# A pooled-attention and mixture-of-experts kernel: another place for the second lane's first weight loads, and a small table made on another engine at another slot

## The chip, the cores and the metric

The kernel runs on one core of one Trainium2 chip. The metric is device time in microseconds of one execution, from the first to the last instruction with what lies around it; less is better.

## The reference

```python
def _attn_ref(q, k, v):            # 8 batches, 8 heads, 576 positions, head size 64
    k_p = k.reshape(B, H, S // 8, 8, D).mean(axis=3)
    v_p = v.reshape(B, H, S // 8, 8, D).mean(axis=3)
    attn = softmax(q @ k_p.T / sqrt(D))
    return attn @ v_p
def _moe_ref(x, w_in, w_out):      # 4608 tokens, 512 -> 2048 -> 512
    h = x @ w_in
    return np.maximum(0.01 * h, h) @ w_out
def _moe2_ref(x, w_gate, w1, w2):  # 8 experts, 512 -> 1024 -> 512
    logits = x @ w_gate
    expert_idx = np.argmax(logits, axis=1)
    gate_w = softmax(logits)[np.arange(N), expert_idx]
    for e in range(E):
        xe = x[expert_idx == e]
        out[expert_idx == e] = gate_w[expert_idx == e, None] * (np.maximum(xe @ w1[e], 0) @ w2[e])
    return out
```

The output of each part, laid out as 4608 tokens of 512 numbers, is the input of the next.

## The kernel before

**Stages.** The tokens go through attention and the dense layer in 18 blocks of 256. The work of a block is 16 slots: in a slot `g1` makes 128 columns of the hidden layer (12 matmuls of 256 columns) and `g2` adds those of an earlier slot to the output (6 matmuls of 512 columns). Each operand is split in a high and a low part, and three of the four products are kept. The first two blocks share 40 slots; while they run, `w_conv1` and `w_conv2` turn the dense weights, which come as 64-bit numbers, into such pairs, on VectorE and ScalarE. All else (attention of later tokens, the routing, the loading and splitting of the experts' weights) is hung on the slots: `at(slot, function)` puts a function in a list, and `run_slot` calls the list of the slot, in the order of the `at` calls, right after the slot's `g1`. The code is written out as each engine's queue, and every engine works through its queue in order.

**Routing.** After each block `route_a` to `route_c` pick the expert of every token and scatter the token's number into a list `lst` in DRAM, by an indirect DMA of GpSimd. `early` picks the expert with most tokens before the last block is counted; four tiles of 128 of its tokens (pairs 0 and 1) start at once.

**The expert stage.** It works on pairs of tiles; a pair has eight slots, again 12 matmuls of 256 columns (`p_g1`) and 6 of 512 (`p_g2`). Slots are counted from 0 anew, so pair p has slots 8p to 8p+7. Weights of experts lie in two lanes of SBUF, four pieces of 2 MB each (`w_load`; pieces 0 and 1 are the first layer, 2 and 3 the second). Pairs 0, 1 and 2 use lane 0, pair 3 is the first that uses lane 1. `w_next` reloads a piece after its last use, with a condition: if the next step of that lane has the same expert, the load is skipped. All these loads are issued by SyncE, in the order of its queue, with the expert's number read from the table `itab` into a register (`value_load`, `w_regs`).

While pair 1 runs, the last block is routed and the plan for the other pairs is made: `final` (slot 5) computes each step's expert with the per-step constants `stepc`; `fetch` (slot 6) reads the token lists; `final_list` (slot 8) writes `itab`; `unpack` (slot 10) makes `gidx`, `sidx` and `gate`, the rows to gather, the rows to write and the factors. Then `p_gather(2)` and `p_gather(3)` issue four indirect gathers on GpSimd, 128 rows each into the two halves of a tile, and `p_xT(2, 0)` and `p_xT(2, 1)` (slots 14 and 15) transpose what came on TensorE, with a copy on ScalarE and a subtraction on VectorE. `m_out` scales a tile's result and scatters it into `out`, by an indirect DMA of GpSimd; a pair has two of them, and the second waits until the first has landed.

**What the change touches.** In slot 8, `final_3` reads the registers of lane 1's first step and issues its pieces 0 and 1. In slot 10, `final_4` issues the four gathers, then has SyncE read one element of `gidx`, and then issues pieces 2 and 3. `step_consts`, in slot 36 of the first stage, makes the six columns of `stepc` from the partition's number: an iota on GpSimd and 29 instructions on VectorE, of one element in each of 128 partitions. `stepc` is read for the first time by `final`.

Of the kernel before, what the change touches and what calls it, by code (L numbers as in the profile page):

```python
# [15 lines left out]
ALU = mybir.AluOpType  # L16
# [5 lines left out]
def kernel(  # L22
# [12 lines left out]
    nc = tc.nc  # L35
    P = 128
    B, H, S, D = q.shape
    NT, DM = out.shape
# [14 lines left out]
    NE = 4  # L53
# [3 lines left out]
    NPS = 12  # L57
    NEP = NE // 2
    FT = NE + 2 * NPS
    NSS = NPS + NSTEP - FT  # L60
# [51 lines left out]
    def sb(shape, dt, tag, bufs=1):  # L112
        return pool.tile(shape, dt, name=tag, tag=tag, bufs=bufs)
# [11 lines left out]
    def f32(ap):  # L125
        return ap.bitcast(F32)
# [4 lines left out]
    def sub(eng, o, a, b):  # L131
        eng.tensor_tensor(out=o, in0=a, in1=b, op=ALU.subtract)  # L132
# [486 lines left out]
    gidx = pool.tile([P, NSTEP], I32, name="gidx")  # L619
# [5 lines left out]
    itab = pool.tile([P, NR + 1, 2], I32, name="itab")  # L625
# [20 lines left out]
    def unpack(L, n, c0):  # L646
        p = pt("att")
        for j in range(2):
            nc.tensor.transpose(p[:, j * 64:j * 64 + n], L[0:n, :, j], ident[0:n, 0:n])
        cs = slice(c0, c0 + n)  # L650
        nc.vector.tensor_copy(sidx[:, cs], p[:, 0:n])
        nc.vector.tensor_scalar(
            out=gidx[:, cs], in0=p[:, 0:n], scalar1=float(NT - 1), scalar2=None, op0=ALU.min
        )
        nc.vector.tensor_copy(gate[:, cs], p[:, 64:64 + n])
# [76 lines left out]
    def final_list(cv):  # L732
        V = nc.vector
        p = pt("att")
        for j in range(2):
            nc.tensor.matmul(
                p[0:1, j * 64:j * 64 + NR], cv[0:NR, j:j + 1], ident[0:NR, 0:NR], start=True, stop=True
            )
        er, ch = etab[0:1], sb([1, NSS], F32, "fch")
        V.tensor_copy(er[:, 2:2 + NPS], p[0:1, 0:2 * NPS:2])  # L740
        V.tensor_copy(er[:, 2 + NPS:2 + NSS], p[0:1, 2 * NPS:NR])
        V.tensor_copy(itab[0:1, 0:NSS, 0], er[:, 2:2 + NSS])
        i = 0
        while i < NSS:
            j = i + 1
            while j < NSS and prev_of(j) - prev_of(i) == j - i:
                j += 1
            a = 2 + prev_of(i)
            V.tensor_tensor(out=ch[:, i:j], in0=er[:, 2 + i:2 + j], in1=er[:, a:a + j - i], op=ALU.not_equal)
            i = j  # L750
        V.tensor_copy(itab[0:1, 0:NPS, 1], ch[:, 0:NPS])
        V.tensor_tensor(
            out=itab[0:1, NPS:NSS, 1], in0=ch[:, NPS:], in1=p[0:1, 64 + 2 * NPS:64 + NR], op=ALU.mult
        )

    def step_consts():
        V = nc.vector
        pi = sb([P, 4], I32, "spi")
        pf = sb([P, 6], F32, "spf")
        j, mem, od, t, x, ns = [pf[:, i:i + 1] for i in range(6)]  # L760
        T, isp, thr, ng, du, c5 = [stepc[:, i:i + 1] for i in range(6)]

        def ts(o, i, a, op0, b=None, op1=None):
            kw = {} if op1 is None else {"op1": op1}
            V.tensor_scalar(out=o, in0=i, scalar1=a, scalar2=b, op0=op0, **kw)

        nc.gpsimd.iota(pi[:, 0:1], pattern=[[0, 1]], base=0, channel_multiplier=1)
        V.tensor_copy(j, pi[:, 0:1])
        ts(pi[:, 1:2], pi[:, 0:1], 1, ALU.bitwise_and)
        V.tensor_copy(mem, pi[:, 1:2])  # L770
        ts(pi[:, 2:3], pi[:, 0:1], 1, ALU.arith_shift_right, 1, ALU.bitwise_and)
        V.tensor_copy(od, pi[:, 2:3])
        ts(pi[:, 3:4], pi[:, 0:1], 2, ALU.arith_shift_right)
        V.tensor_copy(t, pi[:, 3:4])
        ts(isp, j, float(2 * NPS), ALU.is_lt)
        ts(ns, isp, -1.0, ALU.mult, 1.0, ALU.add)
        ts(od, od, float(NPS // 2), ALU.mult)
        V.tensor_tensor(out=t, in0=t, in1=od, op=ALU.add)
        ts(x, j, -2.0 * NPS, ALU.add)
        for q, to in ((4, 6), (5, 4), (6, 7), (7, 5)):  # L780
            ts(od, j, float(2 * NPS + q), ALU.is_equal, float(to - q), ALU.mult)
            V.tensor_tensor(out=x, in0=x, in1=od, op=ALU.add)
        sub(V, t, t, x)
        V.scalar_tensor_tensor(out=T, in0=t, scalar=isp, in1=x, op0=ALU.mult, op1=ALU.add)
        V.scalar_tensor_tensor(out=thr, in0=T, scalar=2.0 * NPS, in1=ns, op0=ALU.add, op1=ALU.mult)
        ts(ng, isp, -1.0, ALU.mult, -1.0, ALU.add)
        ts(du, ns, 2.0, ALU.mult)
        V.tensor_tensor(out=mem, in0=mem, in1=isp, op=ALU.mult)
        V.tensor_tensor(out=c5, in0=T, in1=ng, op=ALU.mult)
        sub(V, c5, mem, c5)  # L790
        ts(c5, c5, -float(E * CAP), ALU.add)
# [47 lines left out]
    def w_load(ln, pieces, e, cond):  # L839
        for pc in pieces:  # L840
            kw = {} if cond is None else {"cond": cond}
            nc.sync.dma_start(
                out=f32(wt[ln, pc].rearrange("p c (h n) -> p c h n", h=2)),
                in_=wsp[bass.ds(e, 1), pc].rearrange("o p c h n -> p (o c) h n"),
                **kw,
            )

    regs = {}

    def w_regs(s):  # L850
        e = nc.sync.value_load(itab[0:1, s, 0:1], min_val=0, max_val=E - 1)
        c = nc.sync.value_load(itab[0:1, s, 1:2], min_val=0, max_val=1) if s < NSS else None
        regs[s] = (e, c)
# [13 lines left out]
    def p_gather(p):  # L867
        x = sb([P, 2, DM], F32, "ps", 3)
        for i in range(2):
            m_gather(2 * p + i, x[:, i])  # L870
# [136 lines left out]
    def at(slot, fn, *a):  # L1007
        hooks.setdefault(slot, []).append((fn, a))
# [97 lines left out]
    with tc.manual_schedule():  # L1106
# [70 lines left out]
            at(o, fn, t)  # L1177
        at(LAG, att_av, 1)
        at(31, prefill)
        at(36, step_consts)  # L1180
        at(20, lambda: nc.sync.dma_start(out=wgk, in_=moe2_w_gate.rearrange("(k p) e -> p k e", p=P)))
        at(27, gate_rows)
        at(4, q_load, 4)
# [16 lines left out]
        for s, (b, f) in enumerate(seq):  # L1200
# [19 lines left out]
            if (b, f) == (1, NF - 1):  # L1220
# [4 lines left out]
                    out=wg_t[0].rearrange("p e d -> p (e d)"),  # L1225
# [26 lines left out]

        def final_3():
            final_list(fin["cv"])
            w_regs(1)
            w_load(1, [0, 1], *regs[1])

        def final_4():
            unpack(early_list.pop(0), NR, NE)
            p_gather(NEP)  # L1260
            p_gather(NEP + 1)
            nc.sync.value_load(gidx[0:1, NE:NE + 1], min_val=0, max_val=NT - 1)
            w_load(1, [2, 3], *regs[1])

        at(0, y_tr, b, 0)
        at(1, y_tr, b, 1)
# [7 lines left out]
        at(5, final_1)  # L1274
        at(6, final_2)
        at(8, final_3)
        at(10, final_4)
        at(14, p_xT, 2, 0)
        at(15, p_xT, 2, 1)
        for p in range(NEP, NEP + NPS):  # L1280
            if p + 2 < NEP + NPS:
                at(8 * p + 1, p_gather, p + 2)
# [86 lines left out]
```

## Time and profile before

| | us |
|---|---|
| median of three runs | 1557.83 (1556.98 to 1558.25) |
| the profiled execution, its own time | 1558.05 |
| its span, first to last instruction | 1556.0 |
| TensorE busy, share of the span | 1472.8, 95% |
| VectorE busy | 939.4, 60% |
| ScalarE busy | 626.8, 40% |
| GpSimd busy | 327.3, 21% |

PE is TensorE's matmuls, PEld its weight loads, DVE is VectorE, ACT ScalarE, POOL GpSimd, SP SyncE; a q behind a name is that engine's sequencer. L900 is line 900 of the kernel. Times in the rows are microseconds from the span's start; the text behind the operation is out<-in by the program's names. A row of the timeline may merge several instructions (x12); its first number is the start of the first, its second reaches to the end of the last. What stands in brackets is the engine's idle time before the row, and what ended it.

### The profile page before, as it was taken

Reading aid. Unit: us, or ns where it says so; the run is one execution under the profiler, and the core shown is the slowest. Engines: PE = TensorE matmul, PEld = TensorE weight load, DVE = VectorE, ACT = ScalarE, POOL = GpSimd, SP = SyncE. Lnnn points to the kernel's source line nnn. Section 1 sums busy time; section 2 is a strip of 40 time slices with the busy share of each in tenths; the row PEclk is TensorE's granted clock in tenths of the full one; section 3 lists DMA queues with packets and bytes.
Section 4 is the critical chain, followed back from the end, with each engine's and each line's share of the span. In section 5 each row is a group of like instructions: output and inputs, shape, how many; then the busy total and the mean of one; then the engine's idle time right before and its main releaser. Section 6 shows DMA issues by size and latency. Waiting matters only on the chain. (4 is left out here: it accounts for less than half of the span.)

```text
span 1556.0 us, 25769 instructions
## 1 busy us (share of the span) xinstructions
PE 1472.8 (95%) x9272; PEld 1317.6 (85%) x9272; DVE 939.4 (60%) x2468; ACT 626.8 (40%) x1442; POOL 327.3 (21%) x294
## 2 busy tenths in 40 slices
PE   3698989999999999999999999999799999999998
PEld 3586879999898888899989989988699999998887
DVE  6998658879778878877877977664122121211111
ACT  4676434544444454444444444322122222222222
POOL 4000012232232233222222332121212111111111
PEclk8699999999999999999999999999899999999999
DMA  9443135555544545535645644143511117566160
GB/s 216 148 132 100 63 99 190 167 188 169 169 167 166 182 149 185 184 140 171 197 153 157 203 149 163 48 178 122 245 41 55 35 48 300 211 257 259 41 250 24
DMA packets 121386, 238.06 MB, mean 153 GB/s; under 512 B 56845, under 2 KB 65041, under 8 KB 117544
## 3 DMA queue, kind: packets, MB, share of 16 engines
q1 hardware_dynamic: 90312, 139.81, 28.7%
q10 hardware_dynamic: 23328, 76.56, 13.0%
q0 software_dynamic: 7616, 20.01, 3.8%
q8 instruction: 75, 1.23, 0.3%
q14 instruction: 55, 0.45, 0.1%
HBM read 317.78 MB, written 87.38 MB: 260 GB/s over the span
## 5 line engine op out<-in xcount | busy, mean ns | idle before, releaser
L526 PE MATMUL y<-w,ghl 128*128 128x512 f32 x1728 | 466.3, 406 | 2.8 <-DVE ghl L132 2.5
L526 PEld LDWEIGHTS y<-w,ghl 128*128 128x128 f32 x1728 | 310.1, 192 | 61.7 <-DVE ghl L132 6.3
L132 POOL TENSOR_TENSOR ps<-ps 128x512 f32<-128x512 f32 x128 | 181.6, 1419 | 482.2 <-ACT ps L129 361.8
L498 PEld LDWEIGHTS h<-x_t,w 128*128 128x128 f32 x1776 | 239.6, 195 | 39.8 <-DVE w L132 16.9
L498 PE MATMUL h<-x_t,w 128*128 128x256 f32 x1776 | 246.4, 288 | 24.0 <-DVE w L132 15.3
L546 DVE CUSTOM_DVE_ANT_0 junk<-y,wg 128x512 bf16<-128x512 f32 x256 | 200.3, 783 | 1.9
L498 PEld LDWEIGHTS y<-x_t,w 128*128 128x128 f32 x1488 | 193.2, 189 | 9.6
L498 PE MATMUL y<-x_t,w 128*128 128x256 f32 x1488 | 196.1, 282 | 0.0
L935 PE MATMUL y<-w,ghl 128*128 128x512 f32 x672 | 176.5, 401 | 0.9 <-DVE ghl L923 0.9
L935 PEld LDWEIGHTS y<-w,ghl 128*128 128x128 f32 x672 | 120.4, 190 | 22.4 <-DVE ghl L923 1.3
L129 ACT ACTIVATE g<-h 128x256 f32<-128x256 f32 x164 | 63.0, 384 | 145.9 <-PE h L498 132.8
L991 POOL DMA_INDIRECT out_dram<-kv,sidx x40 | 40.1, 1003 | 382.5 <-ACT kv L990 199.3
L923 DVE SCALAR_TENSOR_TENSOR ghl<-h,ghl 128x256 fp32r<-128x256 f32 x56 | 23.8, 425 | 135.9 <-ACT ghl L922 135.9
L506 DVE TENSOR_TENSOR h<-g,h 128x256 f32<-128x256 f32 x132 | 56.0, 424 | 77.7 <-ACT g L129 77.2
L132 DVE TENSOR_TENSOR at_t<-a,at_t 128x512 fp32r<-128x512 f32 x62 | 42.7, 688 | 87.6 <-ACT at_t L129 87.2
L129 ACT ACTIVATE ghl<-h 128x256 fp32r<-128x256 f32 x132 | 50.7, 384 | 92.9 <-PE y L526 42.8
L129 ACT ACTIVATE ps<-ps 128x512 fp32r<-128x512 f32 x128 | 80.5, 629 | 17.8 <-DMA ps<-in_moe_w_dram 8.7
L129 ACT ACTIVATE ghl<-y 128x256 fp32r<-128x256 f32 x124 | 47.3, 382 | 95.2 <-DVE y L506 50.5
L132 DVE TENSOR_TENSOR x_t<-a,x_t 128x512 fp32r<-128x512 f32 x60 | 41.1, 688 | 51.7 <-ACT x_t L129 51.7
L129 ACT ACTIVATE g<-y 128x256 f32<-128x256 f32 x124 | 47.4, 382 | 60.9 <-PE y L498 53.4
L295 DVE TENSOR_TENSOR kv<-kv 72x512 f32<-72x512 f32 (+8 forms) x126 | 68.0, 540 | 3.2
L613 POOL DMA_INDIRECT lst<-ent,six x36 | 37.8, 1051 | 150.4 <-DVE six L612 115.1
(291 smaller groups left out, 2157.2 us busy)
## 6 DMA issues: line engine op xcount, KB each, us to landing
w<-wsp SPq DMA_DIRECT2D x108, 2048.0 KB
wsp<-ps ACTq DMA_DIRECT2D x128, 512.0 KB
ps<-in_moe_w_dram SPq DMA_DIRECT2D x128, 256.0 KB
y_d<-y ACTq DMA_DIRECT2D x18, 512.0 KB
q<-in_q_dram SPq DMA_DIRECT2D x28, 256.0 KB
kv<-in_k_dram SPq DMA_DIRECT2D x24, 288.0 KB
kv<-in_v_dram SPq DMA_DIRECT2D x24, 256.0 KB
ps<-in_moe_w_in_dram SPq DMA_DIRECT2D x8, 512.0 KB
```

Of the source, the lines that this page charges most:

```text
L129: nc.scalar.activation(o, i, AF.Copy, scale=scale)
L132: eng.tensor_tensor(out=o, in0=a, in1=b, op=ALU.subtract)
L295: eng.tensor_tensor(out=o, in0=t[:, :, 0:w], in1=t[:, :, w:2 * w], op=ALU.add)
L498: nc.tensor.matmul(p[:, 0:BLK], win(f)[:, kk, l], xv[:, kk, r], start=(n == 0), stop=(n == 3 * KD - 1))
L506: nc.vector.tensor_tensor(out=g, in0=t, in1=h, op=ALU.max)
L526: nc.tensor.matmul(y_ps[b, i], hl[:, l, i * P:i * P + P], wout(f)[:, r], start=(f == 0 and l + r == 0), stop=(last and l == 1),)
L546: nc.vector.tensor_tensor_reduce(out=jk, in0=y_sb[b][:, i], in1=wg_t[0][:, e], scale=1.0, scalar=0.0, op0=ALU.mult, op1=ALU.add, accum_out ...
L613: nc.gpsimd.indirect_dma_start(out=lst, out_offset=bass.IndirectOffsetOnAxis(ap=ix[:, 0:1], axis=0), in_=ent[:, i, :], in_offset=None, bou ...
L923: nc.vector.scalar_tensor_tensor(out=hl[:, 1], in0=b, scalar=0.0, in1=f32(hl[:, 0]), op0=ALU.max, op1=ALU.subtract)
L935: nc.tensor.matmul(o_ps[2 * p + i], hl[:, l, i * P:i * P + P], w[:, r], start=(f == 0 and l + r == 0), stop=(f == 7 and l == 1),)
L991: nc.gpsimd.indirect_dma_start(out=out, out_offset=bass.IndirectOffsetOnAxis(ap=sidx[:, t:t + 1], axis=0), in_=o, in_offset=None, bounds_c ...
```

## The change

Three things are done.

1. `first_load`, a new function in slot 12, takes the place of the four loads in slots 8 and 10. It sets one element of `itab` on VectorE, has SyncE read that element, reads the registers of lane 1's first step and issues all four pieces. In VectorE's queue the new instruction stands right behind the subtraction of `p_xT(2, 0)`. The read of `gidx` goes.
2. `p_xT(2, 0)` moves from slot 14 to slot 12, ahead of `first_load`, and `p_xT(2, 1)` from slot 15 to slot 14.
3. `step_consts` moves from slot 36 to slot 20 of the first stage. Its iota and its first seven VectorE instructions stay on their engines; the other 22 go to GpSimd, where two that did two operations on three operands become two each, so 24.

```diff
         V.tensor_copy(od, pi[:, 2:3])
         ts(pi[:, 3:4], pi[:, 0:1], 2, ALU.arith_shift_right)
         V.tensor_copy(t, pi[:, 3:4])
+        V = nc.gpsimd
         ts(isp, j, float(2 * NPS), ALU.is_lt)
...
         sub(V, t, t, x)
-        V.scalar_tensor_tensor(out=T, in0=t, scalar=isp, in1=x, op0=ALU.mult, op1=ALU.add)
-        V.scalar_tensor_tensor(out=thr, in0=T, scalar=2.0 * NPS, in1=ns, op0=ALU.add, op1=ALU.mult)
+        V.tensor_tensor(out=t, in0=t, in1=isp, op=ALU.mult)
+        V.tensor_tensor(out=T, in0=t, in1=x, op=ALU.add)
+        ts(thr, T, 2.0 * NPS, ALU.add)
+        V.tensor_tensor(out=thr, in0=thr, in1=ns, op=ALU.mult)
...
-        at(36, step_consts)
+        at(20, step_consts)
...
         def final_3():
             final_list(fin["cv"])
-            w_regs(1)
-            w_load(1, [0, 1], *regs[1])
 
         def final_4():
             unpack(early_list.pop(0), NR, NE)
             p_gather(NEP)
             p_gather(NEP + 1)
-            nc.sync.value_load(gidx[0:1, NE:NE + 1], min_val=0, max_val=NT - 1)
-            w_load(1, [2, 3], *regs[1])
+
+        def first_load():
+            nc.vector.memset(itab[0:1, NSS, 0:1], 0.0)
+            nc.sync.value_load(itab[0:1, NSS, 0:1], min_val=0, max_val=1)
+            w_regs(1)
+            w_load(1, range(4), *regs[1])
...
-        at(14, p_xT, 2, 0)
-        at(15, p_xT, 2, 1)
+        at(12, p_xT, 2, 0)
+        at(12, first_load)
+        at(14, p_xT, 2, 1)
```

## Rows read from the trace of the kernel before

**Rows 1.** Waits of TensorE, whole span: total us, times, longest us.
```profile
PE a L900 <- DMA ps<-y_d,gidx: 9.1, 2, 8.8
...
PE h L498 <- DVE ghl L132: 4.5, 2, 4.0
```

**Rows 2.** Timeline of the expert stage while pair 1 runs.
```profile
1085.20 35.97 SPq L842 DMA_DIRECT2D w<-wsp  x8
...
1087.14 1.02 POOL L991 DMA_INDIRECT out_dram<-kv,sidx  x1 [4.83 <-ACT kv L990]
...
1095.06 1.56 PE L935 MATMUL y<-w,ghl 128*128 128x512 f32 x6
...
1097.18 0.98 POOL L991 DMA_INDIRECT out_dram<-kv,sidx  x1 [9.02 <-ACT ghl L922]
...
1098.46 1.05 POOL L876 DMA_INDIRECT ps<-y_d,gidx  x1 [0.30 <-issue]
...
1099.82 1.01 POOL L876 DMA_INDIRECT ps<-y_d,gidx  x1 [0.31 <-issue]
...
1109.63 1.09 PE L900 MATMUL a<-ident,ps 128*128 128x128 f32 x4 [8.76 <-DMA ps<-y_d,gidx]
```

**Rows 3.** Busy time by engine, granted clock, DMA share, GB/s, four microseconds each.
```profile
1108.00:1112.00 4.00, 2.37 (x8) 2.11 (x9) 0.61 (x1) 0.60 (x1) 0.00 (x0) 0.50 0.69 275
1112.00:1116.00 4.00, 4.00 (x23) 3.57 (x23) 0.50 (x2) 0.92 (x2) 0.00 (x0) 0.78 0.00 1
```

**Rows 4.** GpSimd's timeline at the end of pair 1: the second scatter.
```profile
1125.75 0.99 POOL L991 DMA_INDIRECT out_dram<-kv,sidx  x1 [2.65 <-ACT ghl L922]
```

**Rows 5.** Line 876, the gathers, whole span.
```profile
DMA to landing us min/median/max: 3.4/3.9/10.2
```

**Rows 6.** Line 842, the weight loads, whole span: ns min/median/max.
```profile
L842 SPq DMA_DIRECT2D w<-wsp x108: 73/73/358, 1032.5 to 1550.9; - x108
```

**Rows 7.** TensorE's timeline: first matmuls of pair 3.
```profile
1141.57 1.60 PE L914 MATMUL h<-at_t,w 128*128 128x256 f32 x12
```

**Rows 8.** Timeline of the first stage around slot 36.
```profile
213.60 0.15 DVE L768 CAST spf<-spi 128x1 f32<-128x1 int32 x1
...
213.83 1.29 POOL L132 TENSOR_TENSOR ps<-ps 128x512 f32<-128x512 f32 x1 [48.55 <-DVE spi L765]
...
214.34 0.15 DVE L774 CAST spf<-spi 128x1 f32<-128x1 int32 x1
...
215.55 1.55 PE L526 MATMUL y<-w,ghl 128*128 128x512 f32 x6
...
217.86 0.74 DVE L394 TENSOR_REDUCE st<-pr 128x8 f32<-128x576 f32 x1
...
218.64 0.17 DVE L395 TENSOR_SCALAR st<-st 128x8 f32<-128x8 f32 x1
...
221.05 2.93 PE L498 MATMUL h<-x_t,w 128*128 128x256 f32 x12 [3.95 <-DVE ghl L132]
```

**Rows 9.** Busy time by engine and granted clock behind that wait.
```profile
220.00:224.00 4.00, 2.95 (x14) 2.95 (x15) 1.65 (x7) 0.38 (x1) 2.46 (x2) 0.50 0.10 26
224.00:228.00 4.00, 4.00 (x21) 3.45 (x21) 2.85 (x7) 1.99 (x5) 0.91 (x1) 0.71 0.33 133
```

**Rows 10.** Timeline: a short VectorE instruction beside a GpSimd one.
```profile
242.45 1.29 POOL L132 TENSOR_TENSOR ps<-ps 128x512 f32<-128x512 f32 x1 [5.03 <-ACT ps L129]
...
242.95 0.82 DVE L395 TENSOR_SCALAR st<-st 128x8 f32<-128x8 f32 x1
```

**Rows 11.** Busy time by engine and granted clock around slot 20.
```profile
152.00:156.00 4.00, 1.69 (x8) 0.96 (x7) 3.90 (x10) 2.53 (x5) 0.00 (x0) 1.00 0.00 0
```

**Rows 12.** Timeline: the last TensorE wait for VectorE in the conversion of weights.
```profile
163.42 0.66 PE L359 MATMUL a<-ident,q 128*128 128x128 f32 x4 [2.29 <-DVE at_t L132]
```

**Rows 13.** GpSimd's two-input instructions by shape: busy us, mean ns, idle before.
```profile
L295 POOL TENSOR_TENSOR w<-w 128x256 f32<-128x256 f32 x2 | 1.4, 724 | 0.2
...
L295 POOL TENSOR_TENSOR w<-w 128x128 f32<-128x128 f32 x2 | 0.9, 453 | 0.2
```

## The prediction

> **What bounds the kernel now.** I read the page first: TensorE is busy for 95% of the span, so a change can only win where TensorE stands still or runs slowly, or lose where it would be made to. The list of what TensorE waited for, longest first, tells where that is. Two entries belong to the two places that this change touches [rows 1]: the transposes of gathered rows waited 9.1 us for the gather, nearly all of it at once, and the first matmuls of a slot waited 4.0 us at once for VectorE. The timelines around both waits show what came late.
>
> First place, the expert stage. The weight loads of lane 1 start at 1085.20, and GpSimd issues the first scatter of pair 0 at 1087.14 [rows 2]. The second scatter must wait for the first to land, and does so for 9.02 us [rows 2]; at the end of pair 1, where no weights are moving, the same wait is 2.65 us [rows 4]. So the gathers behind it start at 1098.46 instead of some 6 us sooner, and then take long themselves: over the whole kernel a gather lands 3.4 us after its issue at best and 10.2 at worst [rows 5]. TensorE stands still for 8.76 us until 1109.63 [rows 2]. Behind the wait the granted clock is 0.50 and then 0.78, that is 1.2 GHz for part of the time, where it is 2.4 otherwise [rows 3]. In these two stretches TensorE was busy for 2.37 and 4.00 us, so the slow clock cost 2.37 x 0.50 + 4.00 x 0.22 = 2.07 us. The whole loss here is 8.76 + 2.07 = 10.83 us.
>
> Second place, slot 36 of the first stage. TensorE is through with its work at 215.55 + 1.55 = 217.10 and then waits for 3.95 us, because VectorE is working off `step_consts` from 213.60 to 217.86 and only then comes to what TensorE needs [rows 8]. The clock falls here too: 2.95 x 0.50 + 4.00 x 0.29 = 2.64 us [rows 9].
>
> **The change part by part.**
>
> *The weights of lane 1.* Without them nothing large moves from 1085 on. The first scatter still starts at 1087.14; it takes 1.02 us to issue, and its landing should then take the undisturbed wait of 2.65 us [rows 4], so the second starts at 1090.81. The first gather follows 1.28 us behind a scatter and the second gather 1.36 us behind the first [rows 2], at 1092.09 and 1093.45. Undisturbed they land after 3.4 to 3.9 us (the least and the median of all gathers [rows 5]): the first tile's at 1095.5 to 1096.0, the second's at 1096.9 to 1097.4.
>
> *`p_xT(2, 0)` two slots sooner.* Slot 12 comes to TensorE at 1095.06 [rows 2], so there is still a wait. It is 0.4 us if the transposes need only their own tile, and up to 2.3 if they need both halves of the buffer. In the trace TensorE went on at 1109.63, which is 11.2 us behind the first gather's start and 9.8 behind the second's; as no gather took more than 10.2 [rows 5], it was the second that was waited for. I take 2.0 us. A standstill of this size need not bring the slow clock: in the four microseconds from 152 TensorE stood still for 2.31 us and the clock stayed at 1.00 [rows 11]. I take nothing for it here, and price the other case as a rival. Gain of the first place: 10.83 - 2.0 = 8.8 us. The second transposes come a slot later than the first in work and have their data by then.
>
> *The later start of the weights.* The new VectorE instruction waits behind the subtraction of `p_xT(2, 0)`, and SyncE waits for it. Behind SyncE's read stand its four real loads and then lane 0's remaining three conditional loads, which pair 2 needs from its slots 18 and 20 on. These are not delayed much: the usual load instruction takes 73 ns against up to 358 [rows 6], and I read the short ones as skipped, which then move nothing and have nothing to wait for in the queue. The loads themselves: transposes end at about 1097.7, copy and subtraction take about 1.3 us more, the reads of registers about 1.6 (an estimate), so they start near 1101. In the trace the four took from 1085.20 until the DMA share fell to nothing between 1108 and 1112 [rows 2, 3], at most 27 us with the gathers among them. So they are in by 1128. Pair 3 starts at 1141.57 [rows 7], less 8.8 us is 1132.8, and needs only the first piece then. Cost nothing; the cover is 5 us for all four pieces and some 25 for the first. While they run, the scatters of pair 1 and the gathers of pair 4 will be slow in their turn, by about the 6.4 us that 9.02 exceeds 2.65 by; pair 4's rows are needed twelve slots later, over 30 us, so this costs nothing either.
>
> *`step_consts` off VectorE in slot 36.* VectorE can start its next work at 213.60, when it now starts `step_consts`. The reduction takes 0.78 us to the next start [rows 8], so the short L395 would start at 214.38. But GpSimd's subtraction runs from 213.83 to 215.12 [rows 8], and the same L395 beside such an instruction took 0.82 us instead of 0.17, until the GpSimd instruction was over [rows 10]. So it is done at 215.12, and from its start to TensorE's release it is 221.05 - 218.64 = 2.41 us [rows 8]: TensorE is released at 217.5, after 0.4 us of waiting instead of 3.95, and at full clock. Gain 3.95 - 0.4 + 2.64 = 6.2 us.
>
> *What comes to slot 20.* There VectorE is busy for 3.90 of 4 us [rows 11] and TensorE waits for it, for the last time at 163.42 [rows 12]; whatever VectorE loses before that, TensorE loses. Seven instructions stay on VectorE: from 213.60 to 214.34 + 0.15 [rows 8] is 0.9 us. The 24 on GpSimd wait for nobody but VectorE's seven, and nobody waits for them until `final`, 900 us later. But they can hold VectorE up, as in [rows 10]. How long one takes, no row shows. GpSimd's two-input instruction takes 724 ns for 256 columns and 453 for 128 [rows 13]; drawn out to one column this is 0.18 us. So the cost is between nothing (they run beside VectorE) and 24 x 0.18 = 4.3 us (each holds up an instruction for all its length). I take 1.5, a third: VectorE works in part on instructions that read TensorE's results, and part of the 24 should come after 163.42, where nobody waits. Loss 0.9 + 1.5 = 2.4 us.
>
> The Trainium skill speaks against this part: "SBUF — State Buffer", section "Who interferes with whom", says that VectorE and GpSimd share a pair of ports as an exclusive lock, that whoever starts first has it for the whole instruction, and that a VectorE instruction with two inputs in SBUF is shut out by a GpSimd one that reads SBUF. The trace agrees in [rows 10]. By that rule the loss would go to the upper end of 4.3 us and the sum below would be smaller by 2.8.
>
> *Sum.* 8.8 + 6.2 - 2.4 = 12.6 us. The profiled execution took 1558.05, 0.2 us over the median of the three runs; 1558.05 - 12.6 = 1545.45, and I say 1545.5.
>
> **The rivals.**
>
> *The lock costs its full price.* All 24 instructions meet a VectorE instruction and hold it up for 0.18 us: 4.3 instead of 1.5, so 1548.3. For it: VectorE is hardly ever idle there [rows 11]. Against: some of its instructions read TensorE's results, and the 0.18 is mostly start-up. Its far end is the one way to a clear loss: the change without it gains 14.1 us, so at 0.59 us for each of the 24 nothing is left, and at 0.75 each, 18 us, the time would be 1562. That is over four times what [rows 13] give.
>
> *The clock falls in slot 12.* If the second gather lands after 4.5 us instead of 3.5, TensorE stands still for 2.9 us and I charge it the price that the clock had behind 3.95 us of waiting, 2.64 [rows 9]. The first place then gains 10.83 - 2.9 - 2.6 = 5.3 us, and the time is 1549.0. For it: four gathers and two scatters follow closely on one another. Against: it is quiet in the DMA queues then.
>
> *The weights were not what held the gathers.* Then the rows come at 1109.63 as before, TensorE asks for them at 1095.06 already and waits 14.6 us instead of 8.76. That is 5.8 us lost, the other 3.8 are gained: 1560.1, slower than before. The point from which it decides: each microsecond that the rows come after 1097.1 costs one, and at 1109.7 the whole gain is gone. Against it: 9.02 us beside the loads and 2.65 without them, for the same wait [rows 2, 4].
>
> **How the numbers follow.** My forecast, a gain between 10 and 16 us, gets 0.70; the lock at full price 0.13, and its far end 0.03; the fallen clock 0.11; gathers that stay slow 0.03. The low end of the range is the forecast without the lock (1.5), with transposes that wait 0.4 us (1.6) and slot 36 without its rest (0.4): 1542. The high end takes in both middle rivals and most of their sum (1545.5 + 2.8 + 3.5 = 1551.8): 1551. A measurement of this kernel tells about 0.2%, 3 us, from no change. Faster by more gets 0.94, all of the forecast and the two middle rivals; within 0.2% 0.03, the slow gathers; slower 0.03, the lock's far end.
>
> **What the profile after would show.** GpSimd's second scatter some 3.7 us behind the first, the four gathers between 1092 and 1097 less what was gained before, a wait of about 2 us at the transposes in slot 12 with the clock at 1.00, and the weights moving between there and pair 3 with no wait of TensorE for them. Near 217 no wait of several microseconds and no stretch at 0.50. Around slot 20 the 24 GpSimd instructions, and VectorE's two-input instructions beside them longer than before by up to 0.18 us. The prediction is wrong if the wait at the transposes is over 5 us, if TensorE waits for lane 0's or lane 1's weights in pairs 2 or 3, or if the stretch from 150 to 165 grows by more than it gives back in slot 36.

## The result, and the profile after

The changed kernel took 1544.97 us, the median of four executions (1540.41 to 1546.34), against 1557.4 (1555.7 to 1558.25) before on the same chip: a ratio of 0.9916, 95% interval 0.9893 to 0.994. The forecast was 1545.5, with a range from 1542 to 1551. The profiled execution took 1546.34, with a span of 1544.6, 11.4 less than before.

The views are read in the order of the prediction. First what TensorE waited for, over the whole span (total, times, longest). Of the two entries of [rows 1] the one for the gather is gone, and the other is:

```profile
PE h L498 <- DVE ghl L132: 0.9, 2, 0.6
```

Neither long wait is left. The timeline of the expert stage shows how; it answers to [rows 2, 4, 7]:

```profile
1085.35 1.03 POOL L994 DMA_INDIRECT out_dram<-kv,sidx  x1 [4.83 <-ACT kv L993]
1089.01 0.98 POOL L994 DMA_INDIRECT out_dram<-kv,sidx  x1 [2.63 <-DVE gate L655]
1090.29 1.05 POOL L879 DMA_INDIRECT ps<-y_d,gidx  x1 [0.30 <-issue]
1091.64 1.01 POOL L879 DMA_INDIRECT ps<-y_d,gidx  x1 [0.31 <-issue]
...
1093.87 0.63 PE L903 MATMUL a<-ident,ps 128*128 128x128 f32 x4 [0.44 <-issue]
...
1097.88 16.97 SPq L845 DMA_DIRECT2D w<-wsp  x8
...
1121.10 0.99 POOL L994 DMA_INDIRECT out_dram<-kv,sidx  x1 [10.03 <-issue]
...
1129.56 1.60 PE L917 MATMUL h<-at_t,w 128*128 128x256 f32 x12
```

The second scatter now follows the first after 2.63 us of waiting, and the transposes start 3.58 us behind the first gather's start. That is only 2.23 us behind the second gather's start, sooner than any gather lands whose landing [rows 5] give (3.4 us at the least), so the transposes of the first tile did not wait for it. The weights start at 1097.88. It is now pair 1's second scatter that stands behind them, for 10.03 us, and nobody waits for it: pair 3's matmuls start with no wait ahead of them.

The windows of the same stretch (busy time of PE, PEld, DVE, ACT, POOL, then the granted clock, DMA share, GB/s) answer to [rows 3]:

```profile
1092.00:1096.00 4.00, 3.56 (x25) 3.11 (x25) 1.12 (x3) 1.04 (x3) 2.65 (x3) 1.00 0.77 197
...
1104.00:1108.00 4.00, 4.00 (x25) 3.50 (x24) 0.42 (x1) 0.38 (x1) 0.00 (x0) 1.00 1.00 426
```

Around the wait at the transposes the clock is 1.00, and while the weights move at 426 GB/s TensorE is never idle. Slot 36 of the first stage answers to [rows 8 to 10]:

```profile
214.00 1.29 POOL L132 TENSOR_TENSOR ps<-ps 128x512 f32<-128x512 f32 x1 [47.35 <-ACT ps L129]
...
214.55 0.77 DVE L395 TENSOR_SCALAR st<-st 128x8 f32<-128x8 f32 x1
...
217.56 1.70 PE L498 MATMUL h<-x_t,w 128*128 128x256 f32 x12 [0.30 <-DVE ghl L132]
```

L395 takes 0.77 us beside GpSimd's subtraction, as was forecast, and TensorE waits for 0.30 us. In slot 20 the seven instructions stand on VectorE, and GpSimd's come beside VectorE's later work:

```profile
153.43 0.42 DVE L132 TENSOR_TENSOR ghl<-g,ghl 128x256 fp32r<-128x256 f32 x1
153.77 0.15 DVE L768 CAST spf<-spi 128x1 f32<-128x1 int32 x1
...
154.58 0.75 DVE L394 TENSOR_REDUCE st<-pr 128x8 f32<-128x576 f32 x1
...
156.55 0.68 DVE L132 TENSOR_TENSOR w<-kv,w 128x512 fp32r<-128x512 f32 x1
156.63 0.68 POOL L765 TENSOR_SCALAR spf<-spf 128x1 f32<-128x1 f32 x1
...
157.28 2.50 PE L498 MATMUL h<-x_t,w 128*128 128x256 f32 x10 [2.41 <-DVE w L132]
...
177.82 0.60 PE L556 MATMUL a<-ident,wgk 128*8 128x128 f32 x4
```

VectorE's two-input instructions keep their 0.68 us; it is GpSimd's that is long. The trace of before has the same ghl and the same L556 here:

```profile
152.81 0.42 DVE L132 TENSOR_TENSOR ghl<-g,ghl 128x256 fp32r<-128x256 f32 x1
...
177.65 0.60 PE L556 MATMUL a<-ident,wgk 128*8 128x128 f32 x4
```

So the execution after entered slot 20 0.62 us late (nothing is changed ahead of it) and left 0.17 late: by this pair of traces slot 20 gave 0.45. That is the clock of the trace before, and not the change. From this ghl to this L556 the trace before takes 24.84 us. Four runs told of below also keep `step_consts` out of slot 20, and take 23.5 to 23.6; this is `loads_only`:

```profile
153.21 0.42 DVE L132 TENSOR_TENSOR ghl<-g,ghl 128x256 fp32r<-128x256 f32 x1
...
176.75 0.60 PE L556 MATMUL a<-ident,wgk 128*8 128x128 f32 x4
```

The trace after takes 24.39, and so do, to 0.03 us, the three others that run the same code there (`after_again`, `consts_only`, `loads_slot10`). Against these runs slot 20 cost 0.8 us. In the trace before the clock stood at 0.61 in the four microseconds from 164, behind the wait of [rows 12] and with no wait left to hide it; in `loads_only` it stood at 0.57 in those from 156, and TensorE waited for VectorE behind that anyway.

**Where the 11.4 us came from.** The same instruction is found in both traces, and the shift is taken from place to place.

| stretch | shift of its end, us | its own part |
|---|---|---|
| up to slot 20 | +0.62 | 0.6 lost |
| slot 20 to L556 behind it | +0.17 | 0.45 gained |
| slot 36 (matmuls at 221.15, before at 227.03; shift ahead of it +0.16) | -5.88 | 6.0 gained |
| from there to pair 0's first scatter (1085.35, before 1087.14) | -1.79 | 4.1 lost |
| to pair 3 (1129.56, before 1141.57) | -12.01 | 10.2 gained |
| to the end | -11.4 | 0.6 lost |

The 6.0 us of slot 36 hold some of the clock too: from L556 to the matmuls of that row the trace before takes 49.38 us, `loads_only` and `xt_early`, with the same wait of 4 us, 48.57 and 48.58, the trace after 43.33. Against those two the slot gave 5.2.

The 4.1 us that were lost between 227 and 1085 are in no term of the prediction. The windows of that stretch show where they lie. After:

```profile
300.00:320.00 20.00, 19.26 (x115) 17.57 (x115) 12.30 (x36) 9.39 (x22) 5.29 (x4) 0.83 0.40 142
408.00:424.00 16.00, 14.87 (x84) 13.55 (x83) 8.03 (x24) 6.15 (x15) 4.18 (x3) 0.79 0.14 53
784.00:800.00 16.00, 14.32 (x80) 13.08 (x79) 8.19 (x23) 6.79 (x16) 4.53 (x4) 0.79 0.12 42
```

Before, the corresponding places, some 6 us later (from 414 to 430 the clock is 1.00 as well), and one more:

```profile
306.00:326.00 20.00, 19.26 (x136) 17.78 (x136) 14.68 (x43) 10.67 (x26) 5.17 (x4) 1.00 0.51 178
...
650.00:670.00 20.00, 17.82 (x109) 15.83 (x109) 16.70 (x47) 9.95 (x25) 7.54 (x6) 0.91 0.41 136
786.00:806.00 20.00, 18.33 (x119) 16.80 (x118) 13.40 (x41) 9.69 (x23) 5.72 (x5) 0.91 0.36 128
```

A window loses its length times what the clock lacks. After: 20 x 0.17 + 16 x 0.21 + 16 x 0.21 = 10.1 us. Before: 20 x 0.09 + 20 x 0.09 = 3.6. That is 6.5 more. Against it stands a TensorE wait of 2.2 us in the window from 650 of before, which is missing after: 4.3 net, and 4.1 was measured. The work is the same in both; TensorE waited for 0.74 us at the same place in each trace (at 301 after, at 307 before), and only after did the clock fall behind it. One pair of traces can't say how much of this the change brings: over the eleven kept traces with the same code there the stretch takes 855.8 to 867.5 us, 860.1 before and 864.2 after.

### The profile page after: what moved, and what is told of

It reads as the page before. It is cut to its first block, busy times and chain, and to the rows that moved or that the text cites. A ratio compares the mean times of both kernels' runs of the same rounds, so it can differ in the third digit from the quotient of the medians.

```text
span 1544.6 us, 25772 instructions
## 1 busy us (share of the span) xinstructions
PE 1477.1 (96%) x9272; PEld 1321.7 (86%) x9272; DVE 935.9 (61%) x2447; ACT 625.8 (41%) x1442; POOL 336.1 (22%) x318
## 5 line engine op out<-in xcount | busy, mean ns | idle before, releaser
L132 DVE TENSOR_TENSOR ghl<-h,ghl 128x256 fp32r<-128x256 f32 x132 | 55.5, 420 | 24.5 <-ACT ghl L129 24.1
```

## The experiments

Each kernel is the changed one with the edit shown, or the kernel before with part of the change; ratios are to the kernel before, beside it on the same chip.

**Each part alone.** `loads_only` makes the first two edits and leaves `step_consts` in slot 36 on VectorE.

```diff
-        V = nc.gpsimd
...
-        at(20, step_consts)
+        at(36, step_consts)
```

> The kernel before with the change of the weight loads and the transposes alone; step_consts stays in slot 36 on VectorE. My theory, from the traces of before and after: the expert stage gives 8.76 us of waiting and 2.07 us of slow clock back and keeps a wait of 0.4 us, so some 10 us: about 1547 us, with slot 36 as before (a wait of about 4 us near 217). Rival: most of the gain came from step_consts and from chance; then about 1552.

It took 1546.93 us, ratio 0.994 (0.9919 to 0.9961). The long wait at the transposes is gone and slot 36's is there:

```profile
220.16 2.38 PE L498 MATMUL h<-x_t,w 128*128 128x256 f32 x12 [3.96 <-DVE ghl L132]
...
1089.58 0.63 PE L900 MATMUL a<-ident,ps 128*128 128x128 f32 x4 [0.35 <-DMA ps<-y_d,gidx]
```

`consts_only` has the loads and transposes as before, and `step_consts` as changed.

```diff
+            w_regs(1)
+            w_load(1, [0, 1], *regs[1])
...
+            nc.sync.value_load(gidx[0:1, NE:NE + 1], min_val=0, max_val=NT - 1)
+            w_load(1, [2, 3], *regs[1])
...
-        at(12, p_xT, 2, 0)
-        at(12, first_load)
-        at(14, p_xT, 2, 1)
+        at(14, p_xT, 2, 0)
+        at(15, p_xT, 2, 1)
```

> The kernel before with step_consts in slot 20, mostly on GpSimd, and the weight loads as before. My theory: 3.6 us of waiting and 2.6 us of slow clock are gone in slot 36, and slot 20 costs under 1 us: 5 to 6 us, about 1552 us, less what chance falls of the clock take. Rival (the lock costs its full 4.3 us in slot 20): about 1556.

It took 1549.48 us, ratio 0.9954 (0.9938 to 0.9971), and in it the other wait is left:

```profile
216.80 1.70 PE L498 MATMUL h<-x_t,w 128*128 128x256 f32 x12 [0.30 <-DVE ghl L132]
...
1102.88 1.09 PE L903 MATMUL a<-ident,ps 128*128 128x128 f32 x4 [8.78 <-DMA ps<-y_d,gidx]
```

The two parts gain 0.6% and 0.46%, together about what the whole change gains (0.84%), within the intervals. Each removes its own wait and does not touch the other's.

**Was it the weights, or the order of the transposes?** `xt_early` leaves all loads where they were and moves only the transposes.

```diff
-        at(14, p_xT, 2, 0)
-        at(15, p_xT, 2, 1)
+        at(12, p_xT, 2, 0)
+        at(14, p_xT, 2, 1)
```

> The kernel before with only the transposes moved, to slots 12 and 14; the loads stay in slots 8 and 10 and step_consts in slot 36. My theory (the weights held the gathers): the rows come at about 1109 as before, TensorE waits from 1095 on, about 14 us instead of 8.8, and the time is about 5 us more than before, 1562. Rival (the earlier place of the transposes is itself a gain): less than before.

It took 1563.33 us, ratio 1.0041 (1.0027 to 1.0056). The second scatter waits, the first gather comes late, and TensorE, which asks two slots sooner, stands still the longer:

```profile
1093.93 0.98 POOL L991 DMA_INDIRECT out_dram<-kv,sidx  x1 [9.00 <-issue]
1095.21 1.05 POOL L876 DMA_INDIRECT ps<-y_d,gidx  x1 [0.30 <-issue]
...
1106.33 1.09 PE L900 MATMUL a<-ident,ps 128*128 128x128 f32 x4 [14.36 <-DMA ps<-y_d,gidx]
```

This is the time course that the third rival worked out for gathers that stay slow: 14.6 us of wait by its working, 14.36 measured. The same transposes in the same slot wait for 0.35 us in `loads_only`; the one difference is when the weights move.

`loads_slot10` lets the scatters go undisturbed and not the gathers: all four loads are issued in slot 10, as soon as `gidx` is there, with the transposes in slots 12 and 14.

```diff
         def final_4():
             unpack(early_list.pop(0), NR, NE)
             p_gather(NEP)
             p_gather(NEP + 1)
+            nc.sync.value_load(gidx[0:1, NE:NE + 1], min_val=0, max_val=NT - 1)
+            first_load()
...
-            nc.vector.memset(itab[0:1, NSS, 0:1], 0.0)
-            nc.sync.value_load(itab[0:1, NSS, 0:1], min_val=0, max_val=1)
...
-        at(12, first_load)
```

> The kernel after, but all four loads are issued in slot 10 behind the gathers' issue, once SyncE has read gidx, without waiting for rows; transposes in slots 12 and 14. The first scatter of pair 0 has landed by then, the gathers have not. My theory (weights slow the gathers themselves, 10.2 us against 3.5): the transposes wait 6 to 7 us and the clock falls, about 8 us more than the kernel after: 1552. Rival (only the wait between the two scatters was at stake): the same as the kernel after, 1545.

It took 1550.9 us, ratio 0.9964 (0.9947 to 0.998).

```profile
1085.49 0.98 POOL L994 DMA_INDIRECT out_dram<-kv,sidx  x1 [2.63 <-DVE gate L655]
1086.77 1.05 POOL L879 DMA_INDIRECT ps<-y_d,gidx  x1 [0.30 <-issue]
...
1095.44 1.09 PE L903 MATMUL a<-ident,ps 128*128 128x128 f32 x4 [5.53 <-DMA ps<-y_d,gidx]
```

The scatter waits for 2.63 us as in the changed kernel, and then the transposes come 8.67 us behind the gather's start instead of 3.58. So the weights cost in two places: about 6.4 us at the second scatter, and about 5 at the gather. Only the place behind the transposes saves both. By what the loads hold up a scatter or a gather (the queues, the DMA engines, the memory) these runs do not separate.

**The constants: which of slot and engine did it?** `consts20_vector` moves `step_consts` to slot 20 and leaves all of it on VectorE.

```diff
-        V = nc.gpsimd
...
-        V.tensor_tensor(out=t, in0=t, in1=isp, op=ALU.mult)
-        V.tensor_tensor(out=T, in0=t, in1=x, op=ALU.add)
...
+        V.scalar_tensor_tensor(out=T, in0=t, scalar=isp, in1=x, op0=ALU.mult, op1=ALU.add)
...
```

> The kernel after, but step_consts in slot 20 runs wholly on VectorE as it did before (29 instructions, 4.3 us). My theory: in slot 20 VectorE sets TensorE's pace, so the 3.4 us that are more on VectorE are lost: 1 to 4 us more than the kernel after (part may fall on TensorE's slow clock, which costs nothing while it waits). Rival (slot 20 has room on VectorE): the same as the kernel after.

It took 1544.74 us, ratio 0.9915 (0.9894 to 0.9936), which is not to be told from the changed kernel. The trace shows the local loss:

```profile
153.72 0.14 DVE L768 CAST spf<-spi 128x1 f32<-128x1 int32 x1
...
157.85 0.74 DVE L394 TENSOR_REDUCE st<-pr 128x8 f32<-128x576 f32 x1
...
160.55 2.50 PE L498 MATMUL h<-x_t,w 128*128 128x256 f32 x10 [5.73 <-DVE w L132]
...
220.84 1.70 PE L498 MATMUL h<-x_t,w 128*128 128x256 f32 x12 [0.30 <-DVE ghl L132]
```

The reduction comes 4.13 us behind the first cast instead of 0.81, and TensorE waits that much longer, 5.73 us where the changed kernel has 2.41. From the ghl to L556 it takes 27.69 us against 24.39, so TensorE lost all of the 3.3. That GpSimd saves these is read from the trace alone; the times do not show it. The last row is slot 36: its wait is 0.30 us here too.

`consts36_gpsimd` does the reverse: the 24 go to GpSimd, the slot stays 36.

```diff
-        at(20, step_consts)
+        at(36, step_consts)
```

> The kernel after, but step_consts stays in slot 36, with 24 of its instructions on GpSimd. VectorE has 0.8 us more there, and GpSimd's subtraction comes some microseconds later. My theory: the wait near 217 is 1 to 1.5 us instead of 0.3, and slot 20 is 0.8 us cheaper: the same as the kernel after within 1 us. Rival (the slot mattered, not the engine): the wait of 4 us with the slow clock comes back, 5 us more.

It took 1546.76 us, ratio 0.9938 (0.9914 to 0.9962). The times overlap, but the trace contradicts me: the wait of 4 us is back, by another road.

```profile
220.29 1.28 POOL L132 TENSOR_TENSOR ps<-ps 128x512 f32<-128x512 f32 x1
...
222.03 0.63 ACT L129 ACTIVATE ps<-ps 128x512 fp32r<-128x512 f32 x1 [6.18 <-POOL ps L132]
...
224.56 0.42 DVE L132 TENSOR_TENSOR ghl<-h,ghl 128x256 fp32r<-128x256 f32 x1 [7.01 <-ACT ghl L129]
225.03 2.93 PE L498 MATMUL h<-x_t,w 128*128 128x256 f32 x12 [4.03 <-DVE ghl L132]
```

GpSimd works its queue in order too. Its own subtraction for the dense weights stands behind the 24 and comes at 220.29, 6.3 us later than in the changed kernel (214.00); ScalarE waits for it, VectorE for ScalarE, TensorE for VectorE. So the gain of slot 36 came of the other slot: `consts20_vector` has it with all 29 instructions on VectorE, and the other engine by itself does not bring it. What the other engine does is to keep the price in slot 20 at 0.8 us instead of 4.1 (27.69 against the 23.5 to 23.6 without `step_consts`).

**The lock by itself.** The prediction left it between nothing and 0.18 us an instruction. `pool48_short` adds 48 one-column additions on GpSimd to slot 8, where VectorE works without a pause; `pool12_long` adds 12 of 256 columns.

```diff
+    def more_pool():
+        d, s = gate[:, 0:1], gate[:, 1:2]
+        nc.vector.memset(gate[:, 0:2], 0.0)
+        for _ in range(48):
+            nc.gpsimd.tensor_tensor(out=d, in0=d, in1=s, op=ALU.add)
+
+        at(8, more_pool)
```

```diff
+    def more_pool():
+        d = kvn[0][64:128, 4]
...
+        for _ in range(12):
+            nc.gpsimd.tensor_tensor(out=d[:, 0:256], in0=d[:, 0:256], in1=d[:, 256:512], op=ALU.add)
...
+        at(8, more_pool)
```

> The kernel after with one VectorE memset and 48 more GpSimd additions of one column in slot 8, in the stretch in which VectorE is never idle; they do no work for the output. The lock as I priced it (0.18 us each on VectorE): the stretch from slot 8 to slot 20 is 8.6 us longer. What the trace after shows (GpSimd waits, VectorE does not): longer by 0.1 us, and each addition takes 0.4 to 0.7 us instead of 0.2.

> The kernel after with one VectorE memset, one GpSimd memset and 12 more GpSimd additions of 256 columns on 64 partitions in slot 8; they do no work for the output. If VectorE never waits for GpSimd: no longer than the kernel after. If the lock holds for the whole instruction whichever starts first, and short ones only fit in a gap: each holds VectorE up by about 0.6 us, and the stretch from slot 8 to slot 20 is 4 to 8 us longer.

They took 1541.72 us, ratio 0.9899 (0.9869 to 0.9929), and 1545.1, ratio 0.9919 (0.9895 to 0.9943). The first timeline is that of 48 short ones, the second that of 12 long ones:

```profile
99.44 24.84 POOL L760 TENSOR_TENSOR gate<-gate 128x1 f32<-128x1 f32 x48 [72.12 <-DVE gate L758]
...
101.05 0.69 DVE L471 SCALAR_TENSOR_TENSOR ps<-ps 128x512 uint32<-128x512 uint32 x1
...
108.16 0.43 DVE L468 TENSOR_SCALAR r<-r 128x512 uint32<-128x512 uint32 x1
```

```profile
100.00 12.65 POOL L761 TENSOR_TENSOR w<-w 64x256 f32<-64x256 f32 x12
...
101.49 1.10 DVE L471 SCALAR_TENSOR_TENSOR ps<-ps 128x512 uint32<-128x512 uint32 x1
...
113.24 0.43 DVE L468 TENSOR_SCALAR r<-r 128x512 uint32<-128x512 uint32 x1
```

Beside the short ones VectorE's L471 keeps its 0.69 us, and the 48 take 24.84 / 48 = 0.52 us each. Beside the long ones L471 takes 1.10, and the same L468 comes 5.1 us later than beside the short ones: 0.42 us for each of the 12. The stretch that the expectations speak of, from the ghl of slot 8 to that of slot 20, takes 53.91 us in the trace after, 53.94 with the short ones and 59.75 with the long. So GpSimd's instructions do hold VectorE up, and of the two shapes tried only the long one does: for one column VectorE pays nothing that the trace shows, and GpSimd pays.

**The slow stretches between 227 and 1085: chance, or the change?** `after_again` is the changed kernel once more, for its profile and more times. `later_both` puts the constants in slot 29, where the weights are converted and VectorE has idle time, and the transposes and loads in slot 13.

```diff
-        at(20, step_consts)
+        at(29, step_consts)
...
-        at(12, p_xT, 2, 0)
-        at(12, first_load)
+        at(13, p_xT, 2, 0)
+        at(13, first_load)
```

> The kernel after once more, unchanged. If the clock falls behind its waits of 1 to 2 us by chance, this profile has the same waits in the stretch from 250 to 1000 us and another set of slow stretches than the first, and the span differs by half of their difference in length. If the change itself brought the three falls of 6.8 us (near 303, 412 and 788), they are there again. Time: 1545, 1541 to 1547.

> The kernel after with step_consts in slot 29, where VectorE has idle time, and with the first transposes and the loads in slot 13 instead of 12. My theory: VectorE's 0.8 us no longer count, the wait at the transposes of 0.4 us is gone, the loads start one slot later at no cost: about 1 us less than the kernel after, which its time will hardly tell and its trace will. Rival: GpSimd's 24 instructions meet the first weight subtractions or the loads come late for pair 3, and a new wait of 2 us or more shows.

`after_again` took 1541.51 us, the median of nine (1534.84 to 1554.19), ratio 0.9907 (0.9878 to 0.9936). Its windows have the slow stretches in the same three places, with 0.79 from 408 to 424 and from 784 to 800, and here:

```profile
300.00:320.00 20.00, 19.26 (x115) 17.57 (x114) 12.26 (x36) 9.43 (x22) 5.32 (x4) 0.83 0.39 142
```

By what was expected this speaks for the change. But `consts_only` runs the same code up to the expert stage and has the first of these waits, 0.7 us, and not the slow clock behind it:

```profile
300.00:320.00 20.00, 19.29 (x133) 17.82 (x134) 14.46 (x44) 10.73 (x25) 4.53 (x4) 1.00 0.53 184
```

`loads_slot10`, again the same code up to there, has 1.00 in all three places. So the stretch is not fixed by the code ahead of it, and that it came twice in two profiles of the changed kernel is too little to call chance. That the change brings it is not shown either. `later_both` took 1542.25 us, ratio 0.9921 (0.9898 to 0.9944), with no wait at the transposes and with GpSimd's instructions short where VectorE is idle, as it is from 186.84 to 188.84:

```profile
187.54 0.19 POOL L132 TENSOR_TENSOR spf<-spf 128x1 f32<-128x1 f32 x1
...
1092.18 0.60 PE L903 MATMUL a<-ident,ps 128*128 128x128 f32 x4
```

It is cleaner in the trace and not faster by its time: 1541.51 and 1542.25 cannot be told apart.

## Why the prediction was right

The forecast held, and both mechanisms were the ones named; the sum came out partly by luck, as the last point says. Point by point:

- **The weights held the scatter and the gathers: right.** Scatter wait 2.63 us against 2.65 forecast; `loads_only`, `xt_early` and `loads_slot10` show it from three sides, and with them the third rival falls.
- **The wait at the transposes: mis-sized, 0.44 us instead of 2.0.** The step that failed is "it was the second that was waited for". It rested on no gather of [rows 5] having taken over 10.2 us. But the trace gives a landing for only some of the gathers, and among the four of [rows 2] for the last alone. This is what was issued from 1102.3 on, that one gather, with its time to landing:

```profile
ps<-y_d,gidx POOLq DMA_INDIRECT x1, 10.2
```

How long the first one took it does not say, so 11.2 us behind its start excluded nothing. In the changed kernel the transposes ran before the second gather can have landed, so they need their own tile alone, and in `xt_early`, with the same transposes, they started 11.1 us behind the first gather's start. With 0.4 the expert stage is 10.83 - 0.4 = 10.4, and 10.2 was measured. The prediction had named this case as its low bound.
- **The clock behind that wait: right, but not put to the test.** 1.00, so the second rival did not come; the wait was 0.44 us, and the argument was about one of 2.0. Its row was weak besides: the 2.31 us of [rows 11] are no single standstill (the longest wait in that stretch is 1.6 us), and behind the wait of 2.29 us of [rows 12] the clock did fall, to 0.61.
- **Loads behind the transposes cost nothing: right.** They start at 1097.88; the forecast was near 1101, less 1.8 by which the stage began sooner. The scatter that now waits for 10.03 us was forecast at about the 9.02 of [rows 2] and hidden, and so it was.
- **Slot 36: right.** 0.30 us of wait and 0.77 for L395, forecast 0.4 and 0.82. It gave 6.0 us by the pair of traces and 5.2 against the two other runs with the old slot 36, forecast 6.2. What the prediction did not ask is what GpSimd's queue would do if the slot had stayed; `consts36_gpsimd` answers.
- **Slot 20: mis-sized, 0.8 lost instead of 2.4.** VectorE's seven instructions cost it 0.81 us, as forecast (0.9), and TensorE lost that much: 24.39 us from the ghl to L556 against 23.5 to 23.6. So "whatever VectorE loses before that, TensorE loses" held, here and in `consts20_vector`. The term that was mis-sized is the 1.5 for the lock: it was nothing. The 0.45 us gained in the pair of traces are the slow clock of the trace before.
- **The lock at full price: did not come.** Nothing of 24 x 0.18 shows on VectorE. The rule of the Trainium skill, "SBUF — State Buffer", section "Who interferes with whom", that whoever starts first shuts the other out for the whole instruction, agrees with the 12 long ones (0.42 us each on VectorE), two-input instructions such as L471 among them; [rows 10] had shown it on L395 alone, which has one input. For the one-column ones it agrees if VectorE mostly came first: then GpSimd is the one that waits, as its 0.52 us against 0.19 suggests. No row shows who came first for each, so this last is argued.
- **The total was right partly by luck.** Against the other runs the three places gave 5.2 + 10.2 - 0.8 = 14.6 us where 12.6 was forecast: 2.0 too little, 1.6 of it at slot 20 and 1.4 at the transposes, less 1.0 at slot 36. In the pair of traces they gave 0.45 + 6.0 + 10.2 = 16.7, and the stretch between 227 and 1085 took 4.1 of it back, and the ends 1.2. No term of the sum stood for these; they differ from one execution to the next. The second set of times of the same kernel, `after_again`, has a median of 1541.51, 15.4 less than the kernel before beside it and just under the range. What decides whether the clock falls behind a wait of 0.7 us stays open: the same code, with the same wait, has it in two profiles and not in two others.

## What to carry to other kernels

Large loads issued just ahead of a small scatter or gather that TensorE needs soon cost more than their bytes say: look whether the next user of the large data has slack, and start it behind the arrival of the small. When work goes from a full engine to an idle one, read the idle engine's queue as well: what stands behind the moved work there may be what the full engine waits for next. Here GpSimd instructions of one column could be laid beside a busy VectorE at no cost to it, and those of 256 columns could not; sizes between were not tried.

## What had not been expected of the hardware

- Beside VectorE's back-to-back work a one-column GpSimd addition took 0.52 us against 0.19 where VectorE is idle, and VectorE lost nothing; a 64x256 one cost VectorE 0.42 us.
- Behind a wait of TensorE of 0.7 us the clock stood at 1.2 GHz for some 7 us in one execution (20 us at a mean of 0.83) and stayed at 2.4 GHz in another, with the same code ahead of it. Between 230 and 1080 us the kept traces lose some 2 to 12 us in this way. That this is why nine executions of the changed kernel lie as far apart as 1534.84 and 1554.19 is likely and not shown: all but one of them have no trace.
